# Pooling sums on GpSimd, batch 2 in 72 rows, and a third seven-product unit in the first product

## The chip, the cores and the metric

The kernel runs on one core of a Trainium2 chip. The time is the device time of one execution in microseconds (us). The kernel before has a median of 291.4 us in three runs. A run counts as slow when it is over 1.5% above the fastest of its kernel. Faster or slower means by more than 2%.

In this text "tile" means 512 of the 4608 tokens, counted from 0. "First product" is the multiplication by `w_in` for one tile, "second product" the one by `w_out`. TensorE does them one after the other. The timeline gives the start of each, so their lengths can be read as differences of starts.

## The reference, cut to what matters

```python
def _attn_ref(q, k, v):                      # q, k, v: 8 batches, 8 heads, 576 rows, 64
    k_p = k.reshape(B, H, Sp, pool, D).mean(axis=3)      # pool = 8, Sp = 72
    v_p = v.reshape(B, H, Sp, pool, D).mean(axis=3)
    scores = scale * np.matmul(q, k_p.transpose(0, 1, 3, 2))
    # softmax
    return np.matmul(attn, v_p)

def _moe_ref(x, w_in, w_out):                # x: 4608 x 512, w_in: 512 x 2048
    h = x @ w_in
    g = h * (1.0 / (1.0 + np.exp(-h)))       # SiLU
    return g @ w_out
```

The attention output, reordered, is `x`. Each batch needs k and v pooled over 8 neighbouring rows before its attention can run.

## The kernel before

Three parts are touched by the change. The first is the pooling. For batches 3 and later one DMA loads one half of the rows, a second DMA accumulates the other half onto it, and VectorE adds what is left in two steps. Batch 2 comes in another layout, in 128-row slots, and TensorE selects its sums with small matmuls.

```python
    def add_halves(raw):
        nc.vector.tensor_add(
            out=raw[:, :, : 2 * D], in0=raw[:, :, : 2 * D], in1=raw[:, :, 2 * D :]
        )
    def pool_v(b):                                   # pool_k is alike, in two parts
        ...
        add_halves(st["v_raw"])
        add_rest(st["vp"].rearrange("k h (c d) -> k h c d", c=2), st["v_raw"])
```

The second is the unit. A block of `w_in` (512 rows by 512 columns, in quarters) times a tile is done in seven products instead of eight, from sums of quarters. VectorE makes five sums of `x` (`x_sum`), and the intermediate results pass through VectorE and ScalarE:

```python
    UNITS = ((4, 6), (8, 10))
    def unit_x_sum(t, n):
        a, b = U_X[n]
        nc.vector.tensor_tensor(                      # both inputs are in SBUF
            out=x_sum[:, U_XI[n]], in0=x_quarter(t, *a), in1=x_quarter(t, *b), ...
        )
    # stages of a unit (my summary, not in the kernel): 2 -> r_sb (ScalarE); 5 -> rr_sb (VectorE); 1 -> t_sb (VectorE);
    # 4, 3 -> SiLU from PSUM; 7, 6 -> c_sb (VectorE) -> SiLU
            elif n == "5":
                product(y, 5, "Q", True)
                tt(out=rr_sb, in0=ps["Q"], in1=r_sb, op=ALU.add)
            ...
            elif n == "3":
                product(y, 3, "Q", False)             # the next to write bank Q
```

The third is the order. A list of items says how the products of the units and the plain column blocks follow each other in a tile, and "fillers" at numbered steps put work of the other engines in between.

The softmax here doesn't subtract the row's maximum and nothing guards it: scores larger than these inputs give would overflow.

## Time and profile before

| | before |
|---|---|
| median of three runs | 291.4 us |
| TensorE busy | 97% of a span of 288.6 us |
| chain that ended last | TensorE 91% |
| VectorE busy, first product of tile 3 | 12.52 of 13.50 us |
| GpSimd busy | 18% |

TensorE sets the time, at full clock, and VectorE nearly fills the first product. The prediction below shows these lines. The columns are line, engine, operation, output<-inputs, shapes and count, then busy us and mean ns of one, then idle time before:

```profile
L427 DVE TENSOR_TENSOR x_sum<-xT 128x512 bf16<-128x512 bf16 x40 | 14.0, 416 | 0.0
```

Each sum of `x` takes 416 ns. Five of them stand at the head of every tile.

### The profile page before, as it was taken

What the parts mean: (1) busy time and instruction counts of PE and PEld (TensorE: products, weight loads), DVE (VectorE), ACT (ScalarE), POOL (GpSimd) and SP (SyncE); (2) the same over time, 40 slices, a digit from 0 to 9 for tenths busy, and PEclk for the clock granted to TensorE, in tenths of its full rate; (3) what the DMA queues carried; (4) which work ended last, traced back from release to release, by engine and by line L of the source; (5) the groups of instructions that cost most, each with busy time, mean ns of one, the idle gap of its engine ahead of it and who ended that gap; (6) DMA issues with size and microseconds to landing.
All of it is one profiled execution on the core that took longest, in us unless ns stands there. A gap on an engine that the chain in (4) does not pass through costs nothing.

```text
span 288.6 us, 6600 instructions
## 1 busy us (share of the span) xinstructions
PE 281.2 (97%) x2578; PEld 189.9 (66%) x2597; DVE 226.8 (79%) x417; ACT 187.9 (65%) x401; POOL 52.2 (18%) x68
## 2 busy tenths in 40 slices
PE   7989999999999999999999999999999999999995
PEld 2448434465667676657788767676777667786684
DVE  4986844989789796979698879887988876746783
ACT  1768675568656877578767866786679657425700
POOL 8744316501020011101200106203000000000000
PEclk9999999999999999999999999999999999999999
DMA  7999999893758565875995495979830023005004
GB/s 214 276 278 215 232 301 151 221 206 55 145 82 187 127 91 76 133 179 123 137 182 166 61 138 81 164 156 163 149 82 2 2 65 83 1 2 140 6 2 145
DMA packets 35295, 37.67 MB, mean 131 GB/s; under 512 B 9952, under 2 KB 27616, under 8 KB 35264
## 3 DMA queue, kind: packets, MB, share of 16 engines
q0 software_dynamic: 21760, 20.86, 43.3%
q1 hardware_dynamic: 12928, 15.48, 22.0%
q10 hardware_dynamic: 576, 0.92, 0.9%
q8 instruction: 20, 0.33, 0.5%
q14 instruction: 11, 0.09, 0.1%
HBM read 36.70 MB, written 9.44 MB: 160 GB/s over the span
## 4 chain that ended last, share of the span: by engine, by line
PE 91%; DVE 2%; ACT 2%; DMA 2%; issue 1%; DVEq 0%
PE hp_ps L518 24%; PE o_psP L623 15%; PE o_psQ L623 15%; PE u_psQ L460 6%; PE u_psP L460 6%; PE o_psR L623 5%; PE o_ps L550 4%; PE sc_ps L330 4%; PE nu_ps L370 3%; PE den_ps L347 3%; PE u_psR L460 2%; DMA raw<-in_k_dram 2%; PE warm_ps L672 1%; ACT es L338 1%; PE kz_ps L295 1%
## 5 line engine op out<-in xcount | busy, mean ns | idle before, releaser
L518 PE MATMUL hp_ps<-xT,w_in_sb 128*128 128x512 bf16 (+3 forms) x398 | 80.5, 338 | 1.2 <-ACT h_T L524 0.4
L524 ACT ACTIVATE h_T<-hp_ps 128x512 bf16<-128x512 f32 (+2 forms) x95 | 51.4, 545 | 33.1 <-PE hp_ps L518 31.9
L623 PEld LDWEIGHTS <-h_sum 128*128 128x128 bf16 x640 | 60.4, 98 | 15.2 <-issue 6.1
L583 DVE TENSOR_TENSOR h_sum<-h_T 128x1024 bf16<-128x1024 bf16 (+1 forms) x72 | 50.9, 743 | 7.0 <-ACT h_T L524 7.0
L518 PEld LDWEIGHTS <-w_in_sb 128*128 128x128 bf16 x412 | 39.3, 98 | 24.9 <-issue 1.5
L338 ACT ACTIVATE es<-sc_ps 72x288 bf16<-72x288 f32 x128 | 41.4, 402 | 12.6 <-PE sc_ps L330 12.5
L378 DVE TENSOR_TENSOR xT<-nu_ps,rec 128x288 bf16<-128x288 f32 x64 | 25.8, 450 | 13.2 <-PE nu_ps L370 13.0
L460 PEld LDWEIGHTS <-w_sum 128*128 128x128 bf16 x300 | 29.3, 98 | 7.7
L623 PEld LDWEIGHTS <-h_T 128*128 128x128 bf16 x256 | 23.5, 98 | 6.7 <-issue 4.3
L468 ACT ACTIVATE h_T<-c_sb 128x512 bf16<-128x512 f32 x30 | 18.8, 628 | 10.8 <-DVE c_sb L492 10.8
L152 DVE STREAM_TRANSPOSE qT<-q_bf 128x576 bf16<-128x576 bf16 x32 | 22.9, 753 | 0.0
L181 POOL DMA_DIRECT2D raw<-in_k_dram x5 | 7.0, 1405 | 75.1 <-DVE h_sum L583 37.7
L356 ACT ACTIVATE lnd<-den_ps 128x288 f32<-128x288 f32 x30 | 12.3, 411 | 10.8 <-PE nu_ps L370 5.8
L273 DVE TENSOR_TENSOR raw<-raw 128x384 f32<-128x384 f32 (+3 forms) x20 | 12.4, 619 | 8.0 <-DMA raw<-in_v_dram 4.4
L623 PE MATMUL o_psP<-w_out_sb,h_sum 128*128 128x256 bf16 x128 | 17.6, 273 | 0.0
L623 PE MATMUL o_psQ<-w_out_sb,h_sum 128*128 128x256 bf16 x128 | 17.6, 273 | 0.0
L623 PE MATMUL o_psQ<-w_sum,h_T 128*128 128x256 bf16 x128 | 17.5, 274 | 0.0
L623 PE MATMUL o_psP<-w_sum,h_sum 128*128 128x256 bf16 x128 | 17.0, 273 | 0.0
L623 PE MATMUL o_psR<-w_sum,h_sum 128*128 128x256 bf16 x128 | 16.7, 273 | 0.0
L623 PE MATMUL o_psP<-w_sum,h_T 128*128 128x256 bf16 x128 | 16.7, 273 | 0.0
L530 POOL DMA_DIRECT2D out_dram<-o_sb x1 | 0.6, 628 | 82.3 <-issue 82.3
L623 PE MATMUL o_psQ<-w_sum,h_sum 128*128 128x256 bf16 x128 | 15.4, 273 | 0.0
(77 smaller groups left out, 426.8 us busy)
## 6 DMA issues: line engine op xcount, KB each, us to landing
out_dram<-o_sb SPq DMA_DIRECT2D x128, 64.0 KB, 2.5
q_bf<-in_q_dram POOLq DMA_DIRECT2D x6, 576.0 KB, 11.4
raw<-in_k_dram SPq DMA_DIRECT2D x6, 512.0 KB, 5.5
raw<-in_k_dram POOLq DMA_DIRECT2D x5, 576.0 KB, 8.8
raw<-in_v_dram POOLq DMA_DIRECT2D x5, 576.0 KB, 8.7
raw<-in_v_dram SPq DMA_DIRECT2D x5, 512.0 KB, 6.4
w_in_sb<-in_moe_w_in_dram POOLq DMA_DIRECT2D x8, 256.0 KB, 8.7
w_out_sb<-in_moe_w_out_dram POOLq DMA_DIRECT2D x4, 512.0 KB, 13.5
```

The costliest lines, as they stand in the source:

```text
L152: nc.vector.transpose(out=st["qT"][:, a, f * QF : (f + 1) * QF].rearrange("r i c p -> r (i c p)"), in_=st["q_bf"][:, a, f * n : (f + 1) * n],)
L273: nc.vector.tensor_add(out=raw[..., :w], in0=raw[..., :w], in1=raw[..., w : 2 * w])
L330: nc.tensor.matmul(sc[s], lhsT=kz[b % 2][rows, g, c, :], rhs=st["qT"][rows, g, f * QF : (f + 1) * QF, c, :], start=(c == 0), stop=(c == 1),)
L338: nc.scalar.activation(es[:, s, :], sc[s], func=AF.Exp, scale=score_scale)
L356: nc.scalar.activation(lnd, den_ps[:, :HS], func=AF.Ln)
L378: nc.vector.tensor_mul(out=xT[:, 2 * g + c, cols], in0=nu[c][:, :HS], in1=rec)
L460: nc.tensor.matmul(ps[bank][:, u, :], lhsT=w[:, kk, 128 * u : 128 * (u + 1)], rhs=x[:, kk, :], start=first and u == 0 and kk == 0, stop=kk ...
L468: nc.scalar.activation(h_T[:, g : g + 2, j * NQ : (j + 1) * NQ], src, func=AF.Silu)
L518: nc.tensor.matmul(hp_ps[:, r0:r1], lhsT=w_in_sb[:, kk, g * 128 : (g + 1) * 128], rhs=xT[:, kk, x0 : x0 + r1 - r0], start=(kk == 0), stop= ...
L524: nc.scalar.activation(h_T[:, g, n0 : n0 + n], hp_ps[:, :n], func=AF.Silu)
L583: nc.vector.tensor_tensor(out=h_sum[n][:, ks, :], in0=quarter(*a, ks), in1=quarter(*b, ks), op=op)
L623: nc.tensor.matmul(ps[b][:, c, :], lhsT=left(n, kt, c), rhs=W_OUT[n][:, kt, :], start=b not in begun, stop=kt == k1 - 1, skip_group_check= ...
```

## The change

The change moves the pooling sums of k and v from VectorE, which is nearly full, to GpSimd, which is nearly idle. It uses the room for a third unit in the first product of tiles 2 to 8, and it loads batch 2 like the later batches. The diff, cut to its core:

```diff
     def add_halves(raw):
-        nc.vector.tensor_add(
+        nc.gpsimd.tensor_add(
             out=raw[:, :, : 2 * D], in0=raw[:, :, : 2 * D], in1=raw[:, :, 2 * D :]
         )
     def add_rest(dst, raw):
-        nc.vector.tensor_add(
+        nc.gpsimd.tensor_add(
 ...
-    UNITS = ((4, 6), (8, 10))
+    UNITS = ((12, 14), (4, 6), (8, 10))
 ...
-                items = (
-                    G(12, 13) + [(0, "251")] + G(14) + [(0, "43")] + G(15) + [(0, "76")]
-                    + [(1, "2")] + [(0, "s")] + [(1, "51")] + G(0) + [(1, "43")] + G(1)
-                    + [(1, "76")] + G(2) + [(1, "s")] + G(3)
+                items = listed(
+                    "A2 g0 A5 g1 B2 A1 A4 A3 B5 B4 A7 A6 B1 Aa C2 B3 C5 B7 As C4 B6 Ba"
+                    " C1 C3 Bs C7 g2 Ca C6 g3 Cs"
                 )
 ...
-                f_up.append((36 if t > 1 else 45, lambda n=n: hidden_sum(n, 4, 8)))
+                f_up.append((49 if t > 1 else 45, lambda n=n: hidden_sum(n, 4, 8)))
 ...
-            q_at = [15, 16, 17, 49] if t > 1 else ...
+            q_at = [5, 9, 20, 49] if t > 1 else ...
 ...
             elif a + 1 < B:
-                    f_down.append((100, lambda stage=stage: pool_k(a + 1, stage)))
 ...
+                f_up.append((1, lambda: load_one(a + 1, "v")))
+                f_up.append((2, lambda: load_rest(a + 1, "v")))
+                f_down.append((30, lambda: pool_k(a + 1)))
+                f_down.append((31, lambda: pool_v(a + 1)))
```

In the list, A, B and C are the three units, the digit is the product, `a` and `s` are the SiLUs of the two `c_sb`, and `g` is a plain block.

More of the change, by code (lines that the diff above doesn't have):

```diff
@@ L111 @@
     xT = singles.tile([128, KF, NX], BF16, name="xT")
-    w_sum1 = [singles.tile([128, 5, 2, 256], BF16, name=f"w_sum1{n}") for n in range(2)]
+    w_sum1 = [singles.tile([128, 5, 2, 256], BF16, name=f"w_sum1{n}") for n in range(3)]
     x_sum = singles.tile([128, 5, 2, NQ], BF16, name="x_sum")
@@ L172, in load_rows, with load_one @@
             eng.dma_start(out=out[r0:r1], in_=in_[r0:r1])
-    def load_one(b, name):
+    def load_one(b, name, eng=nc.sync):
         st = batches.setdefault(b, {})
         raw = raw_tile(f"{name}_raw", H)
-        load_rows(nc.sync, raw, source(b, name)[:, :, :PH])
+        if eng is nc.sync:
+            load_rows(eng, raw, source(b, name)[:, :, :PH])
+        else:
+            eng.dma_start(out=raw, in_=source(b, name)[:, :, :PH])
         st[f"{name}_raw"] = raw
@@ L196, in add_rest, with pool_k @@
         )
-    def pool_k(b, stage):
+    def pool_k(b):
         st = batches[b]
         raw = st["k_raw"]
-        if stage == 0:
-            add_halves(raw)
-            return
+        add_halves(raw)
         st["kp"] = mid.tile([SP, 2, 2, 4, DH], BF16, tag="kp", bufs=1, name="kp")
@@ L247, with load_slots @@
     }
-    def load_slots(eng, b, name, i0, i1, half=None):
-        es = slice(0, RE) if half is None else slice(half * RE // 2, (half + 1) * RE // 2)
+    def load_slots(eng, b, name, i0, i1):
         src = (k if name == "k" else v)[b].rearrange("h (sp p) d -> (h sp) (p d)", p=POOL)
-        src = src[:, es]
-        how = dict(accum_op=ALU.add) if half else {}
         tiles = row_tiles[name]
-        w = es.stop - es.start
         if i0 == SLOTS:
-            eng.dma_start(
-                out=tiles[1][:REST, SLOTS - SA, :w], in_=src[128 * SLOTS :], **how
-            )
+            eng.dma_start(out=tiles[1][:REST, SLOTS - SA], in_=src[128 * SLOTS :])
         else:
@@ L263, in load_slots, with slot_sums @@
             eng.dma_start(
-                out=tiles[j][:, i0 - SA * j : i1 - SA * j, :w],
-                in_=src[128 * i0 : 128 * i1].rearrange("(i r) e -> r i e", r=128), **how
+                out=tiles[j][:, i0 - SA * j : i1 - SA * j],
+                in_=src[128 * i0 : 128 * i1].rearrange("(i r) e -> r i e", r=128),
             )
-    def slot_sums(name, j, halves=False):
+    def slot_sums(name, j):
         raw = row_tiles[name][j]
         dst = rows5[name][:, SA:] if j else rows5[name][:, :SA]
-        w = RE // 4 if halves else RE // 2
+        w = RE // 2
         while w > D:
@@ L444, in up @@
         step = spread(
-            fillers,
-            sum(
-                KF if len(it) == 3 else 2 * len(it[1].strip("s")) for it in items
-            ),
+            fillers, sum(KF if len(it) == 3 else 2 * (it[1] in "2514376") for it in items)
         )
@@ L454, in product @@
                 tag = "mm" if bank == "R" else "at"
-                ps[bank] = ps_tile([128, 2, NQ], FP32, tag, f"u_ps{bank}")
+                ps[y, bank] = ps_tile([128, 2, NQ], FP32, tag, f"u_ps{bank}")
             w, x = unit_weights(y, n), unit_x(t, n)
@@ L460, in product @@
                     nc.tensor.matmul(
-                        ps[bank][:, u, :], lhsT=w[:, kk, 128 * u : 128 * (u + 1)],
+                        ps[y, bank][:, u, :], lhsT=w[:, kk, 128 * u : 128 * (u + 1)],
                         rhs=x[:, kk, :], start=first and u == 0 and kk == 0,
@@ L464, in product @@
                     )
+            return ps[y, bank]
         def hidden(y, i, j, src):
@@ L475, in stage @@
             if n == "2":
-                product(y, 2, "P", True)
-                nc.scalar.copy(r_sb, ps["P"])
+                nc.scalar.copy(r_sb, product(y, 2, "P", True))
             elif n == "5":
-                product(y, 5, "Q", True)
-                tt(out=rr_sb, in0=ps["Q"], in1=r_sb, op=ALU.add)
+                tt(out=rr_sb, in0=product(y, 5, "Q", True), in1=r_sb, op=ALU.add)
             elif n == "1":
-                product(y, 1, "R", True)
-                tt(out=t_sb, in0=ps["R"], in1=rr_sb, op=ALU.subtract)
+                tt(out=t_sb, in0=product(y, 1, "R", True), in1=rr_sb, op=ALU.subtract)
             elif n == "4":
-                product(y, 4, "P", False)
-                hidden(y, 1, 0, ps["P"])
+                hidden(y, 1, 0, product(y, 4, "P", False))
             elif n == "3":
-                product(y, 3, "Q", False)
-                hidden(y, 0, 1, ps["Q"])
+                hidden(y, 0, 1, product(y, 3, "Q", False))
             elif n == "7":
-                product(y, 7, "P", False)
-                tt(out=c_sb[0], in0=ps["P"], in1=t_sb, op=ALU.add)
+                tt(out=c_sb[0], in0=product(y, 7, "P", False), in1=t_sb, op=ALU.add)
+            elif n == "6":
+                tt(out=c_sb[1], in0=product(y, 6, "Q", False), in1=t_sb, op=ALU.add)
+            elif n == "a":
                 hidden(y, 0, 0, c_sb[0])
-            elif n == "6":
-                product(y, 6, "Q", False)
-                tt(out=c_sb[1], in0=ps["Q"], in1=t_sb, op=ALU.add)
             else:
@@ L503, in up @@
             else:
-                for n in it[1]:
-                    stage(it[0], n)
+                stage(*it)
         for _ in step:
@@ L750 @@
     load_w_out(3)
-    def load_half_2(name, half):
-        for i0, i1 in ((0, SA), (SA, SLOTS), (SLOTS, SLOTS + 1)):
-            load_slots(nc.gpsimd, 2, name, i0, i1, half)
     visits = [(f, g) for f in range(2) for g in range(2)]
@@ L769, with listed @@
         else:
-            G = lambda *gs: [(g, 0, NTT) for g in gs]
+            def listed(text):
+                return [
+                    (int(w[1:]), 0, NTT) if w[0] == "g" else ("ABC".index(w[0]), w[1])
+                    for w in text.split()
+                ]
             if t == 1:
-                items = (
-                    G(12, 13, 14, 15) + [(0, "251")] + G(8) + [(0, "43")] + G(9)
-                    + [(0, "76")] + G(10) + [(0, "s")] + G(11, 0, 1, 2, 3)
-                )
-            else:
-                items = (
-                    G(12, 13) + [(0, "251")] + G(14) + [(0, "43")] + G(15) + [(0, "76")]
-                    + [(1, "2")] + [(0, "s")] + [(1, "51")] + G(0) + [(1, "43")] + G(1)
-                    + [(1, "76")] + G(2) + [(1, "s")] + G(3)
+                items = listed(
+                    "g12 g13 g14 g15 B2 B5 B1 g8 B4 B3 g9 B7 Ba B6 g10 Bs g11 g0 g1 g2 g3"
+                )
+            else:
+                items = listed(
+                    "A2 g0 A5 g1 B2 A1 A4 A3 B5 B4 A7 A6 B1 Aa C2 B3 C5 B7 As C4 B6 Ba"
+                    " C1 C3 Bs C7 g2 Ca C6 g3 Cs"
                 )
@@ L800 @@
         if a < B:
-            q_at = [15, 16, 17, 49] if t > 1 else [24, 25, 26, 49] if t else [82, 84, 86, 88]
+            q_at = [5, 9, 20, 49] if t > 1 else [24, 25, 26, 49] if t else [82, 84, 86, 88]
             if t == 0:
@@ L809 @@
                     f_down.append((37 + 3 * j, lambda j=j: copy_v(1, j)))
-            elif t == 1:
-                for j in range(2):
-                    f_up.append((0, lambda j=j: slot_sums("k", j, halves=True)))
-                    f_up.append((22, lambda j=j: select_k(2, j)))
-                    f_up.append((23, lambda j=j: copy_k(2, j)))
-                    f_down.append((8, lambda j=j: slot_sums("v", j, halves=True)))
-                    f_down.append((40, lambda j=j: select_v(2, j, "at")))
-                    f_down.append((41, lambda j=j: copy_v(2, j)))
-            else:
-                f_up.append((22, lambda: k_transpose(a)))
-                f_down.append((10, lambda: pool_v(a)))
+            else:
+                f_up.append((20 if t > 1 else 22, lambda: k_transpose(a)))
             for n in range(4):
@@ L824 @@
             if t == 0:
-                f_down.append((0, lambda: load_half_2("k", 0)))
+                f_down.append((0, lambda: load_one(2, "k", nc.gpsimd)))
                 f_down.append((0, lambda: load_q(2)))
-                f_down.append((0, lambda: load_half_2("k", 1)))
-                for half in range(2):
-                    f_down.append((31, lambda half=half: load_half_2("v", half)))
-                for y in range(2):
+                f_down.append((0, lambda: load_rest(2, "k")))
+                f_down.append((31, lambda: load_one(2, "v", nc.gpsimd)))
+                f_down.append((31, lambda: pool_k(2)))
+                f_down.append((31, lambda: load_rest(2, "v")))
+                for y in range(3):
                     for n in U_W:
@@ L833 @@
             elif a + 1 < B:
-                for stage in range(2):
-                    f_down.append((100, lambda stage=stage: pool_k(a + 1, stage)))
                 f_up.append((0, lambda: load_q(a + 1)))
+                if t == 1:
+                    f_up.append((0, lambda: pool_v(2)))
                 f_up.append((1, lambda: load_one(a + 1, "k")))
+                f_up.append((1, lambda: load_one(a + 1, "v")))
                 f_up.append((2, lambda: load_rest(a + 1, "k")))
-                f_down.append((11, lambda: load_one(a + 1, "v")))
-                f_down.append((12, lambda: load_rest(a + 1, "v")))
+                f_up.append((2, lambda: load_rest(a + 1, "v")))
+                f_down.append((30, lambda: pool_k(a + 1)))
+                f_down.append((31, lambda: pool_v(a + 1)))
             f_down.append((0, attn_tables))
```

## The prediction

> **What bounds the kernel now.** I read the page first: busy times, then the chain of work that ended last.
>
> ```profile
> PE 281.2 (97%) x2578; PEld 189.9 (66%) x2597; DVE 226.8 (79%) x417; ACT 187.9 (65%) x401; POOL 52.2 (18%) x68
> ...
> PE 91%; DVE 2%; ACT 2%; DMA 2%; issue 1%; DVEq 0%
> ```
>
> TensorE is busy 97% of 288.6 us and is 91% of the chain. Busy is not speed, so the second step is the pace of its matmuls, from the chain in order of time (start, us, what), first in the tile of 512 tokens that starts at 115.78 us (tile 3; tile 0 is the first):
>
> ```profile
> 114.03 1.75 PE o_psQ L623 x16
> 115.78 1.08 PE hp_ps L518 x5
> ...
> 120.92 0.65 PE hp_ps L518 x3
> 121.57 0.45 PE u_psP L460 x4
> 122.02 0.03 DVEq L492
> 122.05 0.45 DVE qT L152 x2
> 122.50 0.14 issue
> 122.64 0.66 DVE c_sb L492
> 123.31 0.02 issue
> 123.33 0.02 ACT h_T L468
> 123.35 0.51 issue
> 123.86 0.58 ACT r_sb L477
> 124.44 0.02 issue
> 124.47 0.70 DVE rr_sb L480
> ...
> 125.21 0.60 PE u_psQ L460 x4
> 125.81 0.86 PE hp_ps L518 x4
> ```
>
> Sixteen matmuls of 256 columns take 1.75 us, 109 ns each; four of 512 take 0.86 us, 215 ns. That is the pace of a stream in which each weight load (98 ns in the groups) hides behind the matmul before it. But the chain leaves TensorE at 122 us: a transpose of q on VectorE delays c_sb, which delays ScalarE's copy r_sb, which delays rr_sb, and the matmul that overwrites that bank starts at 125.21. In the same place of tile 2 TensorE's timeline has the four u_psP before it at 94.38 and the four u_psQ at 95.11, where 4 x 109 ns would give 94.82. So VectorE costs TensorE about 0.3 us in each of these two tiles (from 85.68 and from 115.78). In the later tiles the same stretch has no such break.
>
> The third view is the busy time by stretch, for the first product (x by w_in) of tile 3 and for the whole of tile 5:
>
> ```profile
> 115.70:129.20 13.50, 13.27 (x92) 8.72 (x93) 12.52 (x23) 9.12 (x18) 1.16 (x2) 1.00 0.86 166
> ...
> 175.10:204.60 29.50, 29.42 (x282) 20.73 (x284) 25.47 (x45) 22.07 (x47) 9.54 (x11) 1.00 0.99 143
> ```
>
> Columns are the stretch, its length, then busy us of PE, PEld, DVE, ACT and POOL, the clock, DMA. In the first product VectorE is busy 12.52 of 13.50 us: it is the second bound, and the change adds work to exactly this part. ScalarE, with 9.12, has room. Over a whole tile VectorE has 25.47 of 29.5 us.
>
> **What the skill says.** The Trainium skill, "TensorE: Matmul & The Clock Gate", Back-to-back issue gap, gives 518 cycles for 512 columns and 262 for 256 at 2.4 GHz, 216 and 109 ns: this trace agrees (215 and 109). "GPSIMD Engine Reference", section 3.1, measures 4497 ns for an fp32 add of two tensors of 2048 elements per row on GpSimd, against 2293 ns on VectorE. The trace has no GpSimd add; its VectorE add of 1024 takes 1212 ns, in line with half. "SBUF — State Buffer", Who interferes with whom, says that a VectorE instruction with two SBUF inputs contends with a GpSimd instruction that reads SBUF, and that one then fully blocks the other. The trace before can't show it, since GpSimd only issues DMAs there.
>
> **The change, part by part.** The groups that it moves or adds to:
>
> ```profile
> L480 DVE TENSOR_TENSOR rr_sb<-u_psQ,r_sb 128x512 f32<-128x512 f32 x15 | 10.3, 688 | 5.8 <-ACT r_sb L477 5.8
> ...
> L187 DVE TENSOR_TENSOR raw<-raw 72x1024 f32<-72x1024 f32 x10 | 12.1, 1212 | 0.0
> ...
> L192 DVE TENSOR_TENSOR kp<-raw 72x256 bf16<-72x256 f32 x10 | 3.8, 418 | 0.2
> ...
> L192 DVE TENSOR_TENSOR vp<-raw 72x512 bf16<-72x512 f32 x5 | 3.4, 687 | 0.2
> ```
>
> 1. *Third unit, tiles 2 to 8.* Four plain column blocks (16 matmuls of 512, 16 x 215 = 3.44 us) become seven products (28 of 256, 28 x 109 = 3.05 us). TensorE saves 0.39 us in each of seven tiles: 2.7 us. Nearly all of it is on the path, as TensorE is.
>
> 2. *Batch 2 in 72 rows.* In tile 1 the 24 small matmuls that select k and the 12 that select v go. In TensorE's timeline the former push two matmuls of 512 from 58.64 to 59.62 (1.0 us), the latter take 73.72 to about 74.25 (0.55 us). Four transposes (0.13 us) come in: 1.4 us saved, on the path.
>
> 3. *VectorE.* Out go 2 x 1.21 + 2 x 0.42 + 0.69 = 3.95 us per batch; in come four operations of 0.68 us (rr, t and two c), 2.7 us. Per tile 1.2 us less; but the sums leave the second product and the tile's border, while the new work falls into the first product. There the VectorE work by start-to-start spacing (0.60 us per 512-column operation, 0.335 per x_sum, 0.67 per qT, 0.60 per h_sum of 1024) is: o_sb 0.6, five x_sum 1.7, three qT 2.0, twelve unit operations 7.2, three h_sum 1.8: 13.3 us. TensorE's own time there is 21 x 0.437 + 4 x 0.863 + 0.13 = 12.8 us. The two are level, so order decides.
>
> I walk the order of the changed kernel's instructions for a tile with attention, from its first matmul. VectorE: o_sb at 0.25, x_sum 0.85 to 2.53, qT, rr of the first unit 3.2 to 3.8, qT, t at 4.47, qT, rr of the second at 5.74, c_sb of the first to 7.0. TensorE gets to the third unit's first product at 6.67, and it takes the bank (of five) that this c_sb still reads: it waits till 7.05, 0.4 us. After that I find no further wait: the bank of the third unit's second product is free at 7.6 against 7.9, and the last h_sums (four, after the last SiLU at 14.4) come at 15.1 and 15.7 where the second product needs them at 15.4 and 16.3. Tiles 7 and 8 have no qT and no such wait. So 5 x 0.4 = 2.0 us come back in tiles 2 to 6, where tiles 2 and 3 lose their old 0.3 us each (0.6 us).
>
> 4. *GpSimd.* An estimate from section 3.1: 2.2 ns per element, 3072 elements a batch, 6.7 us, on an engine 18% busy. That time is off the path, as kp and vp are wanted a third of a tile later. For batch 2: its first half of k landed before 44.35 us, the second half takes about 9 us more, the sums 3.4, so kp at 56 to 57; the transposes come at 58.7.
>
> 5. *Five more weight sums in tile 0*, 5 x 0.34 = 1.7 us, lie before a VectorE wait of 4.19 us for v's DMA: free.
>
> Sum: -2.7 - 1.4 - 0.6 + 2.0 = -2.7 us: 288.7. Without the new wait it would be 286.7.
>
> **The rivals.** (a) *The shared port.* The stores on SyncE's queue end 10 to 13 us into a tile (115.15 plus 12.68 in tile 3, and k at 127.93); k and v follow with 5.5 and 6.4 us to landing, then GpSimd issues the accumulating halves at 1.4 us each, with 8.8 and 8.7 us to landing. GpSimd's sums thus run at 26 to 34 us from a tile's start, with tiles 29.3 us long: over the next tile's five x_sum, which have two SBUF inputs. If a 2.2 us add really holds them off, the first unit's fourth product (it waits for rr, and has no slack in my walk: 3.9 against 3.92) and the third unit slip with them: 1 to 2 us a tile in five or six tiles, 5 to 10 us, and 292 to 297. Against it: such blocks need the adds to start first, and short DVE instructions may be what blocks GpSimd. I count it as 1 us in all, in half of the chances more. (b) *A late kp.* Between 2 us (batch 2) and 4 us of slack; if DMA and blocking eat it, TensorE waits in the middle of the first product, 1 to 3 us once. (c) *VectorE's relief pays more than I think.* The second product gets 3.9 us of VectorE time back, tile 1 loses 4 us of sums; if tile 1 (32.2 us; its parts add up to 31.6) also sheds its loss and the wait on the bank is less than 0.4, the time is 286. TensorE cannot give more: 2.7 + 1.4 + 0.6 + 0.5 = 5.2 us is its ceiling, 286.2, and 2% is 285.6. (d) *More loads of weights.* 12 more per tile at 98 ns against matmuls of 109: hidden, as in the units there now.
>
> **Range and chances.** With the 1 us of (a) the sum gives 289.5; I weigh (c) a little more, since the positions of the qT (5, 9, 20) look chosen for this order, and put 288.8. The low end is the ceiling, the high end is (a) in half its strength. Two per cent faster lies above the ceiling, so it has little chance; two per cent slower needs all of (a).
>
> **What would show it.** TensorE's time from tile start to tile start in tiles 7 and 8 0.4 us less (25.1 instead of 25.5), in tiles 2 to 6 about the same to 0.4 less; tile 1 about 1.4 us less; in the chain a visit to c_sb or rr_sb before a u_psP in tiles 2 to 6; VectorE's busy time near 226.8 - 5 x 3.95 + 7 x 2.7 + 2.1 (weight sums) - 4.7 (batch 2's sums and copies) = 223 us; GpSimd adds of about 2.2 us. I am wrong if x_sum spans grow past 0.42 us and the chain names GpSimd or x_sum (a), if k's transposes wait for kp (b), or if the pace of u_ps matmuls exceeds 109 ns (d).

## The result and the profile after

The changed kernel has a median of 303.38 us in four runs (301.72 to 306.5), against 291.28 us for the kernel before in the same rounds (290.86 to 291.49). The ratio is 1.0396, with a 95% interval of 1.0353 to 1.0439: it is slower by 4%. Ratios here are from fast runs of the same rounds, so not quite the ratio of the medians that are quoted.

The profiled run of the changed kernel is the slow one of the four, at 306.5 us (the median of the other three is 302.94). Its mean granted clock was 0.983, where the three fast runs had 0.989, 0.994 and 0.989. So its profile shows somewhat more of one effect than the fast runs do, and I come back to this.

These are lines of the page of the changed kernel: busy times, the granted TensorE clock in 40 slices, the chain, and the two groups that matter.

```profile
PE 287.8 (94%) x2633; PEld 197.7 (65%) x2633; DVE 238.4 (78%) x413; ACT 194.5 (64%) x409; POOL 97.4 (32%) x90
...
PEclk9999999999997999989999999799999999999999
...
PE 53%; DVE 15%; DMA 13%; issue 10%; POOL 5%; ACT 2%; DVEq 0%; POOLq 0%
...
L190 POOL TENSOR_TENSOR raw<-raw 72x1024 f32<-72x1024 f32 x12 | 33.0, 2747 | 37.4 <-DMA raw<-in_k_dram 27.6
...
L422 DVE TENSOR_TENSOR x_sum<-xT 128x512 bf16<-128x512 bf16 x40 | 23.4, 647 | 0.0
```

TensorE fell from 91% to 53% of the chain. VectorE has four instructions fewer and is busy 11.6 us longer. The same 40 `x_sum` take 647 ns instead of 416, which alone is 23.4 - 14.0 = 9.4 us. The clock row, all nines before, has a 7, an 8 and a 7.

Where the time went is read tile by tile, from the starts of the products in TensorE's timeline (us, first product and then second product). I put two of the experiments, explained below, beside the two kernels.

| tile | before | after | 72 rows only | GpSimd only writes |
|---|---|---|---|---|
| 1 | 14.35, 17.67 | 14.76, 18.49 | 13.79, 17.88 | 14.83, 17.03 |
| 2 | 13.48, 16.61 | **16.81**, 17.08 | 13.50, 16.60 | 12.76, 17.20 |
| 3 | 13.49, 16.15 | **17.92**, 17.03 | 13.50, 16.15 | 12.75, 16.74 |
| 4 | 13.23, 16.61 | 12.79, 16.95 | 13.23, 16.39 | 12.79, 16.96 |
| 5 | 12.93, 16.61 | **17.58**, 16.86 | 13.15, 16.39 | 12.75, 16.98 |
| 6 | 12.93, 17.07 | 12.76, 17.43 | 13.15, 16.85 | 12.76, 17.43 |
| 7 | 12.81, 12.27 | 12.62, 12.91 | 13.02, 12.27 | 12.63, 12.90 |
| 8 | 13.02, 12.58 | 12.62, 13.20 | 13.02, 12.58 | 12.63, 13.20 |

The first products of tiles 2, 3 and 5 are 3.3, 4.4 and 4.65 us longer than before, 12.4 us of the 16.1 us between the two profiled spans (304.7 and 288.6). The second products together lose 4.4 us, the other first products gain 0.8. This is the timeline of the changed kernel at the head of tile 3 (start, us, engine, line, operation, then in brackets the idle time before and what ended it):

```profile
121.54 5.43 DVE L422 TENSOR_TENSOR x_sum<-xT 128x512 bf16<-128x512 bf16 x5
122.10 2.52 POOL L190 TENSOR_TENSOR raw<-raw 72x1024 f32<-72x1024 f32 x1
...
124.70 1.32 POOL L195 TENSOR_TENSOR vp<-raw 72x512 bf16<-72x512 f32 x1
...
127.60 0.64 DVE L471 TENSOR_TENSOR rr_sb<-u_psQ,r_sb 128x512 f32<-128x512 f32 x1
...
128.29 1.01 PE L452 MATMUL u_psQ<-x_sum,w_in_sb 128*128 128x256 bf16 x4 [2.72 <-DVE rr_sb L471]
...
130.19 1.06 PE L452 MATMUL u_psP<-x_sum,w_in_sb 128*128 128x256 bf16 x4
```

Five `x_sum` take 5.43 us instead of about 1.75, and the longest single one takes 2561 ns, the length of the GpSimd addition beside it (2.52). Then comes `rr_sb` at 127.60, and only then may TensorE overwrite that bank, for the first unit's third product: it had waited 2.72 us. The last line is a second, separate loss. Four matmuls that elsewhere show 0.60 us show 1.06, at a spacing of 0.85 us instead of 0.437. In tile 5 the wait came in two parts (TensorE's timeline):

```profile
190.24 0.61 PE L452 MATMUL u_psP<-x_sum,w_in_sb 128*128 128x256 bf16 x4 [0.79 <-DVE x_sum L422]
192.50 0.67 PE L452 MATMUL u_psQ<-x_sum,w_in_sb 128*128 128x256 bf16 x4 [1.65 <-DVE rr_sb L471]
```

The windows view confirms that the clock itself had dropped in tile 3. The columns are the stretch, its length, busy us of PE, PEld, DVE, ACT and POOL, then clock, DMA share and GB/s:

```profile
120.80:138.70 17.90, 14.58 (x106) 10.55 (x105) 16.20 (x22) 9.97 (x18) 7.27 (x6) 0.90 0.78 159
155.70:168.50 12.80, 12.80 (x123) 11.48 (x121) 12.15 (x22) 9.64 (x18) 0.00 (x0) 1.00 0.71 151
...
128.20:131.20 3.00, 2.91 (x17) 2.11 (x17) 2.67 (x5) 2.01 (x4) 0.00 (x0) 0.50 1.01 185
```

Tile 3's first product had a mean clock of 0.90, and 0.50 in the 3 us after the wait. Tile 4's has no GpSimd work in it (0.00), a clock of 1.00, and takes 12.8 us. The mean clock was 0.90 in tiles 2 and 5 too (17.1 and 17.5 us long), so in the three hit tiles 0.1 x (17.1 + 17.9 + 17.5) = 5.2 us went to the clock. The trace's clock record has one stretch of 3.41 us at 0.50 in each of them, which gives nearly the same (3 x 3.41 / 2 = 5.1). Against the undisturbed lengths in the last column they are 4.05, 5.17 and 4.83 us longer, 14.05 in all; the other 8.8 us are mostly the waits (2.19 us in tile 2, 0.59 + 2.72 in tile 3, 0.79 + 1.65 in tile 5).

Tiles 4 and 6 escaped by timing. The additions of tile 3's stretch ran from 144.84 to 154.42, and tile 4 began at 155.7, because tile 3 itself had been 5 us late. Tile 4 was of normal length again, so its additions, from 182.36 on, reached into tile 5 at 185.4.

### The profile page after: what moved, and what is told of

Its sections match the earlier page's. It is cut to its first block, busy times and chain, and to the rows that moved or that the text cites. A ratio compares the mean times of both kernels' runs of the same rounds, so it can differ in the third digit from the quotient of the medians.

```text
span 304.7 us, 6721 instructions
## 1 busy us (share of the span) xinstructions
PE 287.8 (94%) x2633; PEld 197.7 (65%) x2633; DVE 238.4 (78%) x413; ACT 194.5 (64%) x409; POOL 97.4 (32%) x90
## 4 chain that ended last, share of the span: by engine, by line
PE 53%; DVE 15%; DMA 13%; issue 10%; POOL 5%; ACT 2%; DVEq 0%; POOLq 0%
PE o_psP L609 12%; PE o_psQ L609 12%; PE u_psQ L452 7%; PE u_psP L452 6%; DMA w_out_sb<-in_moe_w_out_dram 4%; DVE x_sum L422 4%; PE o_psR L609 4%; DVE h_sum L569 3%; DMA w_in_sb<-in_moe_w_in_dram 3%; DMA raw<-in_k_dram 3%; PE hp_ps L504 3%; POOL raw L190 3%; DMA raw<-in_v_dram 2%; PE sc_ps L325 2%; PE den_ps L342 2%
## 5 line engine op out<-in xcount | busy, mean ns | idle before, releaser
L504 PE MATMUL hp_ps<-xT,w_in_sb 128*128 128x512 bf16 (+3 forms) x284 | 55.4, 334 | 0.4 <-ACT h_T L510 0.4
L452 PEld LDWEIGHTS <-w_sum 128*128 128x128 bf16 x440 | 44.1, 101 | 11.0 <-DVE x_sum L422 0.5
L190 POOL TENSOR_TENSOR raw<-raw 72x1024 f32<-72x1024 f32 x12 | 33.0, 2747 | 37.4 <-DMA raw<-in_k_dram 27.6
L510 ACT ACTIVATE h_T<-hp_ps 128x512 bf16<-128x512 f32 (+2 forms) x67 | 34.8, 527 | 15.4 <-PE hp_ps L504 14.5
L504 PEld LDWEIGHTS <-w_in_sb 128*128 128x128 bf16 x284 | 27.1, 98 | 16.3 <-issue 1.5
L461 ACT ACTIVATE h_T<-c_sb 128x512 bf16<-128x512 f32 x44 | 27.6, 628 | 7.7 <-DVE c_sb L479 6.2
L469 ACT COPY r_sb<-u_psP 128x512 f32<-128x512 f32 x22 | 12.8, 584 | 23.7 <-DVE rr_sb L471 11.9
L422 DVE TENSOR_TENSOR x_sum<-xT 128x512 bf16<-128x512 bf16 x40 | 23.4, 647 | 0.0
L452 PE MATMUL u_psQ<-x_sum,w_in_sb 128*128 128x256 bf16 x88 | 13.7, 279 | 6.6 <-DVE rr_sb L471 6.6
L471 DVE TENSOR_TENSOR rr_sb<-u_psQ,r_sb 128x512 f32<-128x512 f32 x22 | 14.8, 674 | 5.4 <-ACT r_sb L469 2.4
L479 DVE TENSOR_TENSOR c_sb<-u_psP,t_sb 128x512 f32<-128x512 f32 x22 | 15.1, 686 | 4.9 <-PE u_psP L452 2.2
```

What stands on the lines that cost most here:

```text
L190: nc.gpsimd.tensor_add(out=raw[:, :, : 2 * D], in0=raw[:, :, : 2 * D], in1=raw[:, :, 2 * D :])
L422: nc.vector.tensor_tensor(out=x_sum[:, U_XI[n]], in0=x_quarter(t, *a), in1=x_quarter(t, *b), op=ALU.subtract if n in (3, 4) else ALU.add,)
L452: nc.tensor.matmul(ps[y, bank][:, u, :], lhsT=w[:, kk, 128 * u : 128 * (u + 1)], rhs=x[:, kk, :], start=first and u == 0 and kk == 0, stop ...
L461: nc.scalar.activation(h_T[:, g : g + 2, j * NQ : (j + 1) * NQ], src, func=AF.Silu)
L479: tt(out=c_sb[0], in0=product(y, 7, "P", False), in1=t_sb, op=ALU.add)
L504: nc.tensor.matmul(hp_ps[:, r0:r1], lhsT=w_in_sb[:, kk, g * 128 : (g + 1) * 128], rhs=xT[:, kk, x0 : x0 + r1 - r0], start=(kk == 0), stop= ...
```

## The experiments

My theory after reading the trace: GpSimd's additions, which read two operands from SBUF, hold off VectorE's `x_sum`, which also has two SBUF inputs; TensorE waits, and its clock then drops for a while. The rivals: the third unit itself costs the time (its order, its load on VectorE), the loads moved by the change do (late `kp` and `vp`), or the layout of batch 2 does. All runs but one gave correct results; the exception is named.

### 1. The third unit with the sums on VectorE

```diff
     def add_halves(raw):
-        nc.gpsimd.tensor_add(
+        nc.vector.tensor_add(
 ... (add_rest alike; v's loads and all sums back at their places of before)
```

> The changed kernel with the sums of k and v back on VectorE at their old places (third unit and batch 2 in 72 rows kept). Theory L (GpSimd's adds lock x_sum out): x_sum back at 0.42 us, no wait of 2 us or more on rr_sb in the first product, clock 1.00, time 287 to 290. Theory D (the tight order of the third unit is itself to blame): still 297 or more.

Measured: 295.87 us (295.59 to 296.74), ratio 1.0165 [1.014, 1.019]. `x_sum` is back at 415 ns and the clock at 1.0. Part of the loss remains without any GpSimd addition, so the shared access is not the whole story. The windows view of this kernel, first product of tile 2, shows why there:

```profile
86.00:99.90 13.90, 12.95 (x107) 9.92 (x104) 13.39 (x25) 9.55 (x18) 0.00 (x0) 1.00 0.83 178
```

VectorE is busy 13.39 of 13.90 us: at their old places the sums of k (85.32 to 87.3 us) stand ahead of the five `x_sum`, and the third product of the first unit then waits 0.95 us for `rr_sb` in this tile and in tile 3. Experiment 10 moves these sums. The second products lose 0.6 us each too, which experiment 4 isolates.

### 2. The sums on GpSimd with two units

```diff
-                    "A2 g0 A5 g1 B2 A1 A4 A3 B5 B4 A7 A6 B1 Aa C2 B3 C5 B7 As C4 B6 Ba"
-                    " C1 C3 Bs C7 g2 Ca C6 g3 Cs"
+                    "g12 g13 B2 B5 B1 g14 B4 B3 g15 B7 Ba B6 C2 Bs C5 C1 g0 C4 C3 g1"
+                    " C7 Ca C6 g2 Cs g3"
 ... (fillers at the steps of before)
```

> The changed kernel with the old two units in the old order (sums on GpSimd kept). L: x_sum still 0.6 us or more on average, but the first product has more slack and less work, so part of the loss stays: 292 to 299. D: all of it is gone, 287 to 289.

Measured: 299.53 us (298.51 to 301.14), ratio 1.0291 [1.0254, 1.0328], `x_sum` 676 ns, clock 0.988. Against the next experiment, which does the sums on VectorE and has them and v's loads at their places of before, that is 299.53 - 290.16 = 9.4 us more, with no third unit present. This pair alone does not separate the engine from the moved loads; experiment 4, which keeps the loads, does. Its first products of tiles 2 and 3 are hit in different degrees (14.64 and 19.28 us). TensorE's timeline there:

```profile
91.31 0.60 PE L452 MATMUL u_psQ<-x_sum,w_in_sb 128*128 128x256 bf16 x4 [1.01 <-DVE rr_sb L471]
...
124.56 1.01 PE L452 MATMUL u_psQ<-x_sum,w_in_sb 128*128 128x256 bf16 x4 [3.00 <-DVE rr_sb L471]
```

After a wait of 1.01 us the matmuls keep their pace. After one of 3.00 us they run at half, and the first product of that tile had a mean clock of 0.82.

### 3. Only the 72 rows

Both edits of 1 and 2: sums on VectorE, two units, and batch 2 loaded like the others.

> Sums on VectorE, two units in the old order, only batch 2 in 72 rows: both theories expect about 1.4 us under the kernel before, 289.5 to 290.5; if kp of batch 2 comes late for its transposes, up to 293.

Measured: 290.16 us (290.11 to 290.64), ratio 0.9968 [0.9953, 0.9983]. This part of the change is good, but for 0.8 us, not for 1.4 (the interval lies below 1). In tile 1, VectorE's and then TensorE's timeline show:

```profile
55.67 1.22 DVE L190 TENSOR_TENSOR raw<-raw 72x1024 f32<-72x1024 f32 x1 [1.40 <-DMA raw<-in_k_dram]
...
70.41 1.05 PE L609 MATMUL o_psP<-w_out_sb,h_sum 128*128 128x256 bf16 x8 [0.67 <-DVE h_sum L569]
```

VectorE waited 1.40 us for the accumulating DMA of k. It was then late with everything, and TensorE lost 0.67 us of the saving in tile 1's second product.

### 4. GpSimd only writes (wrong results on purpose)

Each addition on GpSimd becomes two memsets of its output. Two keep GpSimd busy for somewhat less time than the addition (1.9 us, as a 72x1024 memset took 950 ns) and release the same waiters, but they read nothing. The order, the loads and the third unit are those of the changed kernel. The output is wrong (relative error 0.897).

```diff
-        nc.gpsimd.tensor_add(
-            out=raw[:, :, : 2 * D], in0=raw[:, :, : 2 * D], in1=raw[:, :, 2 * D :]
-        )
+        for _ in range(2):
+            nc.gpsimd.memset(raw[:, :, : 2 * D], 0.01)
```

> Wrong result on purpose: each add of the changed kernel on GpSimd becomes two memsets of its output, so GpSimd keeps its place in the order and its waits but reads no SBUF. L with a lock on reads alone: x_sum back at 0.42 us, time 286 to 289. If GpSimd's writes hold VectorE too, x_sum stays above 0.5 us. Theory Q (sums come late through GpSimd's queue): if memsets take as long as the adds the time stays above 297 with waits on kp or vp.

Measured: 290.26 us (290.18 to 290.92), ratio 0.9973 [0.9956, 0.999], `x_sum` 418 ns, clock 1.0. So 13 us of the changed kernel's time hang on the additions' being additions, which read and add, and not on their place, their loads or their writes. The timeline at the head of tile 3, beside the one above:

```profile
115.81 1.96 POOL L191 MEMSET raw<- 72x1024 f32 x2
...
116.07 1.76 DVE L418 TENSOR_TENSOR x_sum<-xT 128x512 bf16<-128x512 bf16 x5
...
119.18 0.60 PE L448 MATMUL u_psQ<-x_sum,w_in_sb 128*128 128x256 bf16 x4
```

GpSimd is busy over all five `x_sum`, they take 1.76 us, and the third product waits for nothing.

This run also shows the change as it was meant, with its third unit undisturbed, and it is still no faster than the 72 rows alone. The table above gives the account for tiles 2 to 6: the first products gain 2.7 us together and the second products lose 2.9. In tiles 7 and 8, which have no sums or attention to shift, the first product gains 0.39 us, as predicted, and the second loses 0.63. The cause is at the border between the products. These are the timelines of VectorE, ScalarE and TensorE at the end of tile 7's first product in the changed kernel, where the same lengths occur:

```profile
262.90 0.68 DVE L481 TENSOR_TENSOR c_sb<-u_psQ,t_sb 128x512 f32<-128x512 f32 x1
263.50 3.27 DVE L569 TENSOR_TENSOR h_sum<-h_T 128x1024 bf16<-128x1024 bf16 x5
...
263.61 0.63 ACT L461 ACTIVATE h_T<-c_sb 128x512 bf16<-128x512 f32 x1
...
265.02 1.05 PE L609 MATMUL o_psP<-w_out_sb,h_sum 128*128 128x256 bf16 x8 [0.44 <-DVE h_sum L569]
```

The third unit's last `c_sb` comes at 262.90, behind two `h_sum`. Its SiLU follows at 263.61, and the `h_sum` made from it is late for the second product. TensorE's eight matmuls before had started at 263.55 and take 0.875 us, so it stood still for about 0.6 us.

### 5. Each large addition cut in eight

```diff
-        nc.gpsimd.tensor_add(
-            out=raw[:, :, : 2 * D], in0=raw[:, :, : 2 * D], in1=raw[:, :, 2 * D :]
-        )
+        for h in range(H):
+            nc.gpsimd.tensor_add(
+                out=raw[:, h, : 2 * D], in0=raw[:, h, : 2 * D], in1=raw[:, h, 2 * D :]
+            )
```

> The changed kernel with each add of 72x1024 on GpSimd cut into eight of 72x128 (one head each, about 0.3 us). If the port is held for a whole instruction, x_sum waits at most about 0.3 us at a time: five x_sum in 2.5 to 4 us instead of 4.2 to 5.4, and 293 to 300. If the two engines merely share bandwidth while both run, nothing changes: 302 or more.

Measured: 302.78 us (301.81 to 303.04), ratio 1.0399 [1.0374, 1.0424]. The groups:

```profile
L191 POOL TENSOR_TENSOR raw<-raw 72x128 f32<-72x128 f32 x96 | 49.4, 544 | 34.4 <-DMA raw<-in_k_dram 18.3 <-DMA raw<-in_v_dram 8.0 <-PE nu_ps L366 4.5
...
L423 DVE TENSOR_TENSOR x_sum<-xT 128x512 bf16<-128x512 bf16 x40 | 22.4, 622 | 0.0
```

An addition of an eighth takes 544 ns on average (the median is 449, and some beside VectorE's work take 629 or more), so eight cost 4.35 us instead of 2.75. Each `x_sum` now waits briefly: in tile 3 all five take 599 to 672 ns, none 2561; the longest of the run, 1486 ns in tile 4, met the `vp` addition, which was not cut. The first products of tiles 2 to 6 become 13.95 to 14.47 us, without the peaks of 17 and 18. But all of them are hit now, and `vp` came 2.49 us too late for tile 1, whose second product took 21.19 us. Shorter additions spread the damage and add their own. The time fell where the expectation had put shared bandwidth (302 or more), but the five `x_sum` of tiles 1 to 6 take 2.80 to 3.50 us together, inside the 2.5 to 4 foreseen for an access held by one instruction at a time. TensorE's timeline also has two waits that are used below:

```profile
78.31 0.43 PE L366 MATMUL nu_ps<-es,vp 72*32 72x288 bf16 x8 [2.49 <-POOL vp L196]
...
95.38 0.60 PE L453 MATMUL u_psQ<-x_sum,w_in_sb 128*128 128x256 bf16 x4 [1.55 <-DVE rr_sb L472]
```

The first was followed by half clock (0.50 from 80.04 to 83.45 us), the second by full clock.

### 6. Loads of k and v on GpSimd's queue

The additions run late because the loads start behind the stores of the output. Here they start earlier, so that the additions end before the next tile begins.

```diff
-                f_up.append((1, lambda: load_one(a + 1, "k")))
-                f_up.append((1, lambda: load_one(a + 1, "v")))
+                f_up.append((1, lambda: load_one(a + 1, "k", nc.gpsimd)))
+                f_up.append((1, lambda: load_one(a + 1, "v", nc.gpsimd)))
```

> The changed kernel with the first halves of k and v of batches 3 on issued from GpSimd's queue at the start of a tile, not behind the stores on SyncE's. L: the adds move from the next tile's start into the second product, where VectorE has slack; x_sum near 0.42 us, waits on rr_sb gone, 290 to 293. If what costs is GpSimd adding at any time (h_sum held in its place), still 297 or more.

Measured: 308.59 us (306.02 to 308.9), ratio 1.058 [1.0526, 1.0633]. The half that I hoped for came: tiles 4 to 6 are clean, with first products of 12.80, 12.76 and 12.88 us. But tile 2's took 21.61 us, because its `kp` was late (the rival of the prediction, here made by my edit), and tile 3's 19.55 us, with additions over `x_sum` again. Tile 2 is of use all the same, for its wait has nothing to do with `x_sum`. TensorE's timeline:

```profile
98.53 0.30 PE L222 MATMUL kT_ps<-shifts,kp 72*128 72x72 bf16 x2 [6.66 <-POOL kp L195]
...
99.73 1.06 PE L452 MATMUL u_psP<-x_sum,w_in_sb 128*128 128x256 bf16 x4
100.59 1.06 PE L452 MATMUL u_psP<-x_sum,w_sum 128*128 128x256 bf16 x4
```

After 6.66 us of waiting for another thing the matmuls again run at half pace, and the clock from 98.5 to 102.2 us was 0.51. The drop followed TensorE's standing still here too, as it did after the wait for `vp` in experiment 5; so it is not tied to `x_sum` or `rr_sb`.

### 7. The same with another end of the first product

```diff
-                    " C1 C3 Bs C7 g2 Ca C6 g3 Cs"
+                    " C1 C3 Bs C7 C6 Ca g2 Cs g3"
```

> The same with the third unit's sixth product moved ahead of the column block g2, so that the last SiLU of a unit is not the last of all. In tiles 7 and 8 of the write-only run the first product is 0.39 us shorter than with two units, but the second 0.63 us longer, as it waits for the last h_sum. If that order is the cause, the second product is back at 12.3 us in tiles 7 and 8, and the time is 3 to 4.5 us under the run before this one; if the wait comes from VectorE's amount of work, nothing changes.

Measured: three fast runs of 306.21 to 308.41 us, ratio 1.0566 [1.0525, 1.0606], no different from experiment 6. The profiled run was slow, 404.27 us at a clock of 0.657, and its profile can't be compared with a fast one's. For the question of the end of the first product this run is inconclusive.

### 8. Early loads, and batch 2's sums on VectorE

Experiment 7 with batch 2's sums on VectorE, at other steps (100 and 20 of tile 1's second product), so that `kp` of tile 2 is in time, and one late `h_sum` moved from step 71 of the second product to 40.

```diff
-        add_halves(raw)
+        eng = nc.vector if b == 2 else nc.gpsimd
+        add_halves(raw, eng)
 ...
-            f_down.append((71, lambda: hidden_sum(6, 0, 4)))
+            f_down.append((40, lambda: hidden_sum(6, 0, 4)))
```

> The same, with batch 2's sums on VectorE and one h_sum earlier in the second product: tile 1 loses its waits on kp and vp (some 2 us). 286 to 289 if all of it adds up; as the run before if tile 1's waits are hidden or the adds now meet x_sum of tile 2.

Measured: 301.57 us (299.83 to 302.66), ratio 1.0358 [1.0311, 1.0406]. Tile 2 is mended (14.53 us), and tile 3 is not: its first product took 22.33 us, since batch 4's additions, from 118 to 126 us, fell on the `x_sum` of this tile, which began at 117.3. TensorE waited 5.39 us there for `rr_sb`. Tiles 4 and 5 are at 13.23 and 16.55 us, 29.8 together, and tile 6 at 30.3, about the same as with three units undisturbed (29.7, 29.7 and 30.2 in experiment 4). In tile 7 the wait of the second product is gone (12.31 instead of 12.90), but the first became longer (13.03 instead of 12.63). Tile 8 gained nothing in its second product (13.21, with a new wait of 0.57 us) and lost as much in its first.

### 9. The third unit in tiles 7 and 8 alone

Experiment 3 with three units only where no attention, and no sums, share VectorE, and with the sixth product of the third unit ahead of the last two plain blocks.

```diff
+                    ... if t < 7 else
+                    "A2 g0 A5 g1 B2 A1 A4 A3 B5 B4 A7 A6 B1 Aa C2 B3 C5 B7 As C4 B6 Ba"
+                    " C3 C1 Bs C7 C6 Ca g2 Cs g3"
```

> Batch 2 in 72 rows, all sums on VectorE, two units except in tiles 7 and 8, where nothing of attention runs; there the third unit, with its third and first product exchanged and its sixth moved ahead of g2. In the combined run the sixth product waited 0.25 us and more for the SiLU of the third, which the exchange should take away. If the unit's arithmetic gain is real once order is right: 12.6 us of first product and 12.3 of second in both tiles, 0.8 us under rows72_only: 289.4. If a wait only moves again: 290.2.

Measured in five rounds: 290.91 us (289.47 to 292.92), ratio 0.9985 [0.9941, 1.0028]. Tile 7 takes 13.00 + 12.35 = 25.35 us, where it takes 13.02 + 12.27 = 25.29 with two units. TensorE needs 0.39 us less and gets nothing of it. ScalarE's and TensorE's timelines:

```profile
245.00 0.58 ACT L461 ACTIVATE h_T<-u_psQ 128x512 bf16<-128x512 f32 x1
...
245.63 0.60 PE L452 MATMUL u_psQ<-x_sum,w_sum 128*128 128x256 bf16 x4
```

The sixth product writes the bank that the third product's SiLU reads until 245.58. It starts at 245.63, 0.62 us after the product before it instead of 0.437. What the other order lost after the border, this one loses ahead of it.

### 10. Three units, all sums on VectorE, k loaded earlier

The order of experiment 9 in tiles 2 to 8, all sums on VectorE, k's first half loaded from GpSimd's queue, and k's sums at step 72 of the second product instead of 100, so that they leave the first product alone.

```diff
-                f_up.append((1, lambda: load_one(a + 1, "k")))
+                f_up.append((1, lambda: load_one(a + 1, "k", nc.gpsimd)))
-                f_down.append((100, lambda: pool_k(a + 1)))
+                f_down.append((72 if t > 1 else 100, lambda: pool_k(a + 1)))
```

> No sums on GpSimd at all: three units from tile 2 on in the new order, k's sums on VectorE in the middle of the second product (its first half loaded early from GpSimd's queue), v's where they were before. If units_vector_sums lost its 5 us to k's sums at the tile border and to the late last h_sum, both are gone: 286.5 to 289. If VectorE simply has too much to do with three units, 291 to 295.

Measured in five rounds: 291.64 us (291.34 to 292.09), ratio 1.0009 [0.9978, 1.0039]. This mends experiment 1 (295.87 us) almost wholly: the first products of tiles 3 to 6 are 13.23 us, the second of tiles 4 and 5 16.55. Tile 2, where the sums of k stay where they were, still takes 14.37 us. So the third unit is nearly harmless when the sums lie elsewhere on VectorE, but it brings nothing: 29.78 us in tile 5, against 29.54 with two units (experiment 3). The time fell in the range that the expectation had given to a VectorE with too much to do; the next experiment speaks against that reading.

### 11. The same with k's sums of batches 4 to 7 on GpSimd, away from `x_sum`

```diff
+        eng = nc.gpsimd if b > 3 else nc.vector
-                f_down.append((72 if t > 1 else 100, lambda: pool_k(a + 1)))
+                f_down.append((30 if t > 1 else 100, lambda: pool_k(a + 1)))
```

> The same with k's sums of batches 4 to 7 on GpSimd, timed to run at 22 to 27 us of a tile, away from x_sum. L says that GpSimd's adds are free when no VectorE operation with two SBUF inputs is near: x_sum 0.42 us, time equal to k_early or up to 1.5 us less. If adds on GpSimd cost VectorE whenever they run, it is slower than k_early by 1 us or more.

Measured in five rounds: 292.65 us (291.67 to 293.67), ratio 1.0042 [1.0008, 1.0076]. With the additions early in the second product, `x_sum` takes 435 ns on average, and only tile 6's first product is touched (14.01 us, the others 13.22 to 13.24 from tile 3 on). The collision can thus be nearly avoided. What remains is that k's sums (1.21 + 2 x 0.42 = 2.05 us per batch) were no bottleneck on VectorE in experiment 10: moved away, they shorten the second products of tiles 3 to 5 by 0.15 us each and the kernel not at all. It is 1.0 us slower than experiment 10, just where the expectation had put additions that cost VectorE at any time; the profiles, 0.3 us apart, show no such cost away from `x_sum`, and the rest of the difference is not explained.

No version beat experiment 3, which is 0.3% faster than the kernel before.

## Why the prediction was wrong, point by point

The time on record was 288.8 us, with (a) "in half its strength" as its high end; measured were 303.4. **The step that failed is the weighing of rival (a), the shared port**, "1 to 2 us a tile in five or six tiles", which went into the sum as "1 us in all". The mechanism, the place (additions at 26 to 34 us from a tile's start, over the next tile's five `x_sum`) and the victim (the first unit's product that waits for `rr_sb`; it is its third, not its fourth) were named. Experiment 4 shows the mechanism: with writes in place of the additions, 13 us go away. The full strength of (a) had been put at 5 to 10 us, and the waits of the profiled run, 8.8 us, lie in it. So the size was wrong twice, in the chance given to the waits and in what follows them:

- *The wait.* Two arguments were held against the rival: that additions might not start first, and that short VectorE instructions might be what blocks GpSimd. In fact several additions follow each other at the head of a tile, and one after another held an `x_sum`, up to 2561 ns. Where it hit, it cost some 3 us in a first product, in tiles 2, 3 and 5, and TensorE's own wait for `rr_sb` was 2.19 us in tile 2, 2.72 in tile 3 and 1.65 in tile 5.
- *The clock.* This was in no part of the prediction. After those waits TensorE ran at half clock for about 3 us, 1.7 us lost in each hit tile, 5.2 in the profiled run. It follows the wait, for `kp` and `vp` too (experiments 6 and 5). In these traces single waits of up to 1.55 us were followed by full clock and waits of 2.19 us and more by half, but so was tile 5's of 1.65 us, which came soon after another of 0.79. The fast runs of the changed kernel had clocks of 0.989, 0.994 and 0.989, so by the same arithmetic (span x (1 - clock)) they lost 3.3, 1.8 and 3.3 us. At 1.7 us for each 3.41 us of half clock, I take it, as an estimate, that they had two, one and two such stretches, instead of three; two can belong to one wait, as after the 3.00 us of experiment 2 (6.83 us at half clock).

So the length of one wait does not decide on the drop. The clock record suggests what does: between the drops of the changed kernel the clock is full for 30.72 and 61.44 us, 9 and 18 times 3.41. I cut each trace (the slow one of experiment 7 left out) into stretches of 3.41 us from the first rise of its clock. Every drop then falls on the end of a stretch. All stretches in which TensorE stood still for 2.0 us or more ended in half clock, and none at full clock with 1.6 us or less did; in between, one with 1.68 us did and two with 1.84 and 1.85 us, at the very end of kernels, did not. This is read from the traces afterwards and was not tested.

The other steps of the sum:

1. *Third unit, 2.7 us saved: the matmuls' time was right, the gain failed.* The pace is 109 ns as foreseen and the first product is 0.39 us shorter in tiles 7 and 8. "The last h_sums ... come at 15.1 and 15.7 where the second product needs them at 15.4 and 16.3" is the failed step. The last `c_sb` stood behind two `h_sum`, and TensorE stood still for 0.6 us at the border of tile 7; the second products of tiles 2 to 8 are all 0.57 to 0.63 us longer. Undisturbed (experiment 4 against 3), the third unit comes to +0.24 us in each of tiles 7 and 8 and, with the sums off VectorE, to +0.04 on average in tiles 2 to 6, where -0.39 was foreseen. With other orders it comes to +0.06 (tile 7, experiment 9) and +0.24 (tile 5, experiment 10).
2. *Batch 2 in 72 rows, 1.4 us saved: right in kind, and about 0.8 in size* in the timed runs. The selections are gone, but in the trace of experiment 3 tile 1's first product is only 0.56 us shorter, where 1.0 - 0.13 = 0.87 was computed. The 1.0 us was misread: the block around k's selections took from 58.42 to 60.06 us instead of 4 x 0.215, so 0.78 more. VectorE's wait of 1.40 us for k and the late `h_sum` of tile 1 (0.67 us) were left out. In the changed kernel `vp` of batch 2 was late too, by 1.39 us, because its addition, beside VectorE's work, took 5.35 us.
3. *The wait of 0.4 us on the bank in tiles 2 to 6: did not occur.* In experiment 4 the first products there take 12.75 to 12.79 us, 0.12 to 0.16 more than in tiles 7 and 8, about the time of k's transposes. The walk put TensorE on a bank that `c_sb` still reads. The timeline of tile 3 has that product at 121.93, 0.44 us after the one before it: full pace. The old 0.3 us in tiles 2 and 3 did go away. So this part erred to the slow side by 2.0 us, and it hid the error in part 1.
4. *GpSimd's additions of 2.2 ns per element: right.* An undisturbed 72x1024 addition took 2.35 us, estimated were 2.25. "Off the path" was wrong.
5. *Five weight sums for free:* tile 0 is equally long, to 0.1 us, in both kernels; right.

Rival (c), relief of VectorE that pays more, is refuted by experiment 4, which takes every sum of batches 2 to 7 from VectorE and still ends at 290.26 us, and by experiment 11. Rival (d), more weight loads, did not show: the pace holds. Rival (b), a late `kp`, was a wait of 0.7 us in tile 1 (batch 2's `kp` was done at 59.8 us, not at 56 to 57); it became large only in experiment 6. Two slips of the prediction changed nothing: 288.7 + 1 is 289.7, not 289.5, and besides DMAs the trace before has six small GpSimd instructions (1.2 us in all). The two rivals of the experiments are settled likewise: the third unit costs 5.7 us when VectorE keeps the sums at their old places (295.87 - 290.16), but it is not what made the changed kernel slow, since with write-only GpSimd work the same order takes 290.26 us.

What stays open is which of the waits made the clock drop in the fast runs of the changed kernel, which have no timeline.

## What to carry to other kernels

Moving work to an idle engine was not free here, because its additions held off instructions of another engine that read two SBUF inputs. Before such a move, list which instructions of VectorE have two SBUF inputs at that time, and assume that each can wait for a whole addition. Stops of TensorE of some 2 to 3 us within a few us cost another 1.7 us each here, through the clock. And a saving of matmul time counts only after the last result has passed VectorE and ScalarE to the next product; follow that border first, then count matmuls.

## What the Trainium skill lacked or had wrong

- "SBUF — State Buffer", Who interferes with whom: right, and it deserves more weight than I gave it. Two-input `x_sum` went from 416 to 647 ns on average and to 2561 at most beside GpSimd additions, and stayed at 418 ns beside GpSimd memsets, which only write. The page has no figure for cutting the addition up: eight short ones took 544 ns each on average and the `x_sum` of tile 3 still lost about 0.2 us each (599 to 672 ns), with no gain in all (302.78 us).
- "TensorE: Matmul & The Clock Gate", Part 1: The HAM clock gate, puts the drop to half clock after an idle window of about 3.4 us. Here waits of 2.19, 2.49, 2.72 and 3.00 us were followed by it (a granted clock of 0.50 in the 3 us after the 2.72 us wait), and so was one of 1.65 us that came after another of 0.79; waits of 1.01, 1.39 and 1.55 us were not. In the 3.41 us before each drop within these kernels TensorE stood still for 1.68 to 3.41 us, so it need not be idle for the whole of them.
- "GPSIMD Engine Reference", section 3.1, held: 2.35 us for 1024 fp32 additions per row, in line with its 4497 ns for 2048. It has no figure for short ones; 128 per row took 449 ns in the median here (544 on average), where an eighth of 2.35 us would be 0.29.
